# Causal scores in steps of four PSUM banks with one exponential each, two heads sharing a diagonal column, and a new instruction order

## The chip, the core and the metric

The kernel runs on one core of one Trainium2 chip. The core has a matrix engine (TensorE, PE in the profile; its weight loads are PEld), a vector engine (VectorE, DVE), an activation engine (ScalarE, ACT), a general engine (GpSimd, POOL) and a queue of DMA transfers issued by SyncE (SP). Matrix results land in PSUM, which the kernel uses as eight banks of 128 partitions x 512 floats; operands lie in SBUF. Each engine executes its own list of instructions in the order in which the program gives them and waits at an instruction whose operand another engine has not yet finished. The metric is the device time of one execution in microseconds, lower is better, as the median of several runs.

## The reference

Two layers of the same kind run over 2048 tokens of width 512: attention with a compressive memory, then a gated feed-forward network (FFN). The sequence is cut into four segments of 512 tokens, with 32 heads of width 16. Inside a segment attention is causal; what came before enters through a memory matrix per head. The same weights are used in both layers.

```python
def _A_ref(x, wq, wk, wv, wo, beta):
    ...
    mask = (ar[:, None] < ar[None, :]) * -1000000000.0
    g = _sigmoid(beta)
    for s in range(N):
        qs, ks, vs = (q[:, :, s], k[:, :, s], v[:, :, s])
        logits = jnp.einsum('bhqd,bhkd->bhqk', qs, ks) * scale + mask
        a_dot = jnp.einsum('bhqk,bhkd->bhqd', _softmax(logits), vs)
        pq = phi(qs)                       # where(t > 0, t + 1, exp(t))
        num = jnp.einsum('bhld,bhde->bhle', pq, M)
        den = jnp.einsum('bhld,bhd->bhl', pq, z)[..., None] + 1e-06
        outs.append(g * (num / den) + (1.0 - g) * a_dot)
        M = M + jnp.einsum('bhld,bhle->bhde', phi(ks), vs)
        z = z + jnp.einsum('bhld->bhd', phi(ks))
    return o @ wo

x = x + _A_ref(_layernorm(x), ...)
x = x + (_gelu(x1 @ w_gate) * (x1 @ w_up)) @ w_down      # x1 = _layernorm(x)
...                                                       # the same two lines again
```

## The kernel before, in words

**Units of work.** Four segments in two layers make eight units, k = 0 to 7 (`NK`). Unit k first projects its 512 tokens to `q`, `kf` (the keys) and `vaug` (the values with a 17th column for the softmax denominator), then forms causal scores, exponentials and weighted sums, adds the memory part, multiplies by wo, and runs the FFN (wg, wu, wd). The memory state goes from unit to unit, and unit k + 4 needs the finished rows of unit k.

**How the matrix engine is cut.** Dense products (`product`, line 458) run as four instructions on four column strips of 32, so four weight loads and four matmuls make one product of 512 columns. Score matmuls (line 893) use the array in four strips of 32 rows instead, one head in each: even heads read `kf`, odd heads read `kB`, a copy of the odd heads' keys in rows whose other half is zero, so that both kinds contract over their own head only. A change between the two ways of cutting the array is a change of tiling; the planner books `SWITCH` for it. The weighted sums (line 957, called a flush here) are cut into column strips like the dense products.

**Score steps.** The 512 x 512 causal square of one head is covered by four tiles of 128 keys, with 512, 384, 256 and 128 query columns, each tile starting at its diagonal block. Four heads (one parity of the eight heads of a block b of 128 features) go side by side. `steps_of` (line 88) packs the tiles into steps of 512 columns for four heads: 20 steps for each unit (`STEPS`). A step writes 4 x 512 columns in PSUM, in two halves of two banks each (`st0` and `st1`, double use of four fixed banks); `scores` (line 872) can issue both halves together or one half alone. Each half has its own exponential on ACT (line 924, 128 x 1024) into a tile `pt`, and then POOL sets the upper triangle of each diagonal block to zero (line 911). The other four banks (`M_BANKS`) serve all other results.

**Flushes.** When all steps of a head group are exponentiated and masked, `flush_item` (line 932) multiplies `pt` with `vaug`; DVE transposes the result (line 981), divides by the denominator and transposes back.

**The order.** `tc.manual_schedule` is on for all engines: the kernel itself writes out each engine's list. It does so with a planner (`Clocks`, `Engine`, line 123 on, and the loop at line 1316): booked clocks of PE, ACT, DVE, POOL and SP with booked costs, a stock of items (`items`) sorted by due times (`DUE`, `DUE_STEP`, `BIAS`), and score steps that go first whenever their operands and banks are there. Where score steps remain and nothing else is ready, the planner emits a filler: a product of the constant tile `warm` (line 1347), whose result nobody reads. The lists are fixed when the program is built; on the chip each engine goes through its list in order.

**The start.** Lines 355 to 409 fill constants on POOL (`kB` memset at line 401, then `cden` at line 402), 19 matmuls of `warm` run on PE (line 366), and lines 1183 to 1252 write the first normalization, transposes and projections by hand. The POOL list there is: constants, `kB` memset, `cden`, then the scale factors of the first normalization (lines 1196 and 1198).

```python
    def product(out, lhsT, rhs, start=True, stop=True):
        ck.tiling("columns")
        for c in range(4):
            r = slice(32 * c, 32 * c + 32)
            nc.tensor.matmul(out[r], lhsT=lhsT[:, r], rhs=rhs, start=start, stop=stop, tile_position=(0, 32 * c))
```

Of the kernel before, what the change touches and what calls it, by code (L numbers as in the profile page):

```python
# [12 lines left out]
ALU = mybir.AluOpType  # L13
# [5 lines left out]
P = 128  # L19
# [17 lines left out]
STEPS = 20  # L37
BY_PE = {("xnTf", 0), ("xnTf", 1), ("xnTf", NK - 1)}
M_BANKS = 4
PT_STEPS = 5  # L40
SETS = 3
WO, WG, X2, WU, X3, WD = 32.0, 37.0, 14.0, 49.8, 27.0, 94.0
# [4 lines left out]
RAW = 7  # L47
QK_DUE = 0.63
E_Q = -0.37
E_K = 0.716  # L50

FLUSH_WAIT = 6.233
PIECE_SLACK = 1.684
URGENT, SOON, NORMAL = -13.08, -0.462, 0.0
EXP_SLACK, E_SLACK, PHI_SLACK, GELU_SLACK = -2.653, 5.546, 3.783, 2.306
ACT_EVICT, FIRST_EVICT = 0.747, 1.76
XN_BUFS = 4
XN_KEPT = 1
XNA1_PE = 0
E_BUFS = 2  # L60
KB_SLACK = 6.407
# [4 lines left out]
MEM_SLACK = 2.5  # L66


DUE = {"wo": 0.775, "gate": 1.026, "up": 1.341, "down": 1.966, "upd": 0.168, "mem": -0.012, "v": 0.072}
DUE_STEP = {"gate": 0.0137, "up": 0.0202, "down": 0.0455}  # L70
BIAS = {
    **{("qk", k): d for k, d in {0: -0.002, 1: 0.026, 2: 0.13, 3: 0.245, 4: 0.171, 5: 0.126, 6: 0.152, 7: 0.076}.items()},
    **{("mem", k): d for k, d in {0: -0.153, 1: -0.371, 2: -0.114, 3: -0.034, 4: -0.306, 5: 0.161, 6: 0.219, 7: 0.053}.items()},
    **{("down", k): d for k, d in {0: 0.142, 1: -0.173, 2: -0.121, 3: -0.112, 4: 0.005, 5: -0.01, 6: -0.141, 7: -0.221}.items()},
    **{("upd", k): d for k, d in {0: -0.053, 1: 0.405, 2: -0.034, 3: 0.527, 4: -0.125, 5: 0.428, 6: 0.107, 7: 0.051}.items()},
    **{("v", k): d for k, d in {0: 0.15, 1: 0.067, 2: 0.083, 3: 0.486, 4: -0.214, 5: -1.018, 6: -0.01, 7: 0.119}.items()},
    **{("wo", k): d for k, d in {0: 0.143, 1: 0.12, 2: -1.173, 3: -0.74, 4: -0.064, 5: -0.385, 6: 0.174, 7: -0.079}.items()},
    **{("gate", k): d for k, d in {0: 0.569, 1: -0.096, 2: -0.084, 3: 0.003, 4: -0.147, 5: 0.268, 6: -0.122, 7: 0.068}.items()},
    **{("up", k): d for k, d in {0: 0.098, 1: 0.239, 2: 0.148, 3: -0.035, 4: 0.01, 5: -0.013, 6: -0.468, 7: -0.065}.items()},
# [7 lines left out]

def steps_of(k):


    if k not in SPLIT:
        found = []
        for b in range(KT):
            if k == b == 0:
                found += [([(b, par, 0, 0, HALF, HALF * par) for par in range(2)], []),
                          ([(b, par, 0, HALF, L, HALF * par) for par in range(2)], []),
                          ([(b, 0, 1, P, L, 0), (b, 0, 3, 3 * P, L, 3 * P)], []),
                          ([(b, 0, 2, HALF, L, 0), (b, 1, 2, HALF, L, HALF)], [(b, 0, None)]),
                          ([(b, 1, 1, P, L, 0), (b, 1, 3, 3 * P, L, 3 * P)], [(b, 1, None)])]
                continue  # L100
            found += [([(b, 0, 0, 0, L, 0)], []),
                      ([(b, 0, 1, P, L, 0), (b, 0, 3, 3 * P, L, 3 * P)], []),
                      ([(b, 0, 2, HALF, L, 0), (b, 1, 2, HALF, L, HALF)], [(b, 0, None)]),
                      ([(b, 1, 0, 0, L, 0)], []),
                      ([(b, 1, 1, P, L, 0), (b, 1, 3, 3 * P, L, 3 * P)], [(b, 1, None)])]
        return found
    found = []
    for b in (0, 2):
        wide = [[(c, par, 0, 0, HALF, HALF * par) for par in range(2)] for c in (b, b + 1)]
        narrow = [(c, par, 1, P, HALF, P * (2 * (c - b) + par)) for c in (b, b + 1) for par in range(2)]  # L110
        found += [(wide[0], []), (narrow, [(b, None, 0)]), (wide[1], [(b + 1, None, 0)])]
    for b in (0, 2):
        last = [(c, par, 3, 3 * P, L, P * (2 * (c - b) + par)) for c in (b, b + 1) for par in range(2)]
        for c in (b, b + 1):
            for par in range(2):
                found.append(([(c, par, 0, HALF, L, 0), (c, par, 1, HALF, L, HALF)], []))
            found.append(([(c, par, 2, HALF, L, HALF * par) for par in range(2)], [(c, None, 1)] if c > b else []))
            if c == b:
                found.append((last, [(b, None, 1)]))
    return found  # L120
# [53 lines left out]
class Clocks:  # L174
# [4 lines left out]
    SWITCH = 0.102  # L179
# [108 lines left out]
def kernel(  # L288
# [69 lines left out]

    def bank_tile(i, shape, dtype=F32):
        return psp.tile(shape, dtype, tag=f"m{i}", bufs=1, name="m")  # L360
# [28 lines left out]
    bdg = cst.tile([P, 4, P], F32, name="bdg")  # L389
    macc = cst.tile([P, 4, P], F32, name="macc")  # L390
    zacc = cst.tile([P, 4], F32, name="zacc")
    kBs = [cst.tile([P, KT, L], BF16, name=f"kB{i}") for i in range(SETS)]
    vaugs = [cst.tile([P, TPS, VW + 15], BF16, name=f"vaug{i}") for i in range(SETS)]

    def by_head(va):
        return va[:, :, 0:VW].rearrange("p t (h e) -> p t h e", e=DH + 1)
# [6 lines left out]
    for va in vaugs:  # L403
        nc.scalar.activation(out=by_head(va)[:, :, :, DH], in_=cden[:].unsqueeze(1).to_broadcast([P, TPS, H]),
                             func=ACT.Copy)
# [5 lines left out]
    def later_constants():  # L411
# [7 lines left out]
        for b in range(4):  # L419
            ck.pool.post(20.0 + 3.0 * b, MEM_SLACK, (0.5, lambda b=b: scale(b), None))  # L420

# [961 lines left out]
```

## Time and profile before

| what | value |
|---|---|
| time, median of 3 runs | 558.17 us (556.5 to 558.3) |
| span of the profiled execution, first to last instruction | 555.8 us |
| TensorE busy in the span | 547.5 us, 99% |
| ACT / DVE / POOL busy | 447.8 / 434.5 / 233.3 us |
| granted TensorE clock, all slices | 9 tenths or more |
| DMA, mean over the span | 50 GB/s |

The profiled execution is one execution; its span is the time between its first and last profiled instruction, and the measured time of a run also contains what lies around that, about 2.4 us here between the span and the median. Times in the fences are microseconds unless marked ns. In a view of groups the columns after the bar are the busy time of the group, the mean duration of one instruction in ns, and the idle time of the engine before them with what ended it. In a timeline the columns are the start, the duration of a merged piece, the engine, the line, the operation and how many instructions were merged. Matmuls overlap in the pipeline, so that the durations of successive pieces overlap too; what one piece costs is the distance between its start and the start of the next.

### The profile page before, as it was taken

To read this page: it belongs to the slowest core of one execution; us is meant where nothing else is said; L and a number is where in the kernel's file an instruction comes from. 1 tells how busy PE (TensorE), PEld (TensorE's weight loads), DVE (VectorE), ACT (ScalarE), POOL (GpSimd) and SP (SyncE) were. 2 spreads that over 40 slices of the span, in tenths; PEclk is the share of its full clock that TensorE was granted. 3 is DMA by queue.
4 is the path that set the end of the run, shared out by engine and by line. 5 is a ranking of instruction groups with operands and counts; after the bars stand their busy time and mean duration, and the time that the engine had idled before them with its cause. 6 is when DMAs were issued, how large, how long until landed. Compare 5 with 4: busy or idle time off the path is not lost.

```text
span 555.8 us, 25686 instructions
## 1 busy us (share of the span) xinstructions
PE 547.5 (99%) x11557; PEld 272.5 (49%) x11557; DVE 434.5 (78%) x820; ACT 447.8 (81%) x544; POOL 233.3 (42%) x470
## 2 busy tenths in 40 slices
PE   8999999999999999999999999999999999999997
PEld 4433344444454444444444444544454444545996
DVE  5978797999969898687967889489876898587161
ACT  5899999987998878987898978988889877973500
POOL 5675664255624455144632555155632562021000
PEclk9999999999999999999999999999999999999999
DMA  7248710610152024220230205101320104020001
GB/s 228 40 107 220 150 25 13 168 37 2 22 60 50 12 31 69 40 41 2 41 50 12 42 2 86 33 16 28 79 59 3 22 13 87 3 22 31 14 4 40
DMA packets 65261, 27.87 MB, mean 50 GB/s; under 512 B 54720, under 2 KB 64704, under 8 KB 65152
## 3 DMA queue, kind: packets, MB, share of 16 engines
q1 hardware_dynamic: 65008, 26.23, 23.3%
q8 instruction: 90, 1.47, 1.1%
q14 instruction: 19, 0.16, 0.1%
q10 hardware_dynamic: 144, 0.01, 0.0%
HBM read 9.71 MB, written 2.10 MB: 21 GB/s over the span
## 4 chain that ended last, share of the span: by engine, by line
PE 88%; DVE 6%; DMA 2%; POOL 1%; ACT 1%; issue 1%; SPq 0%; ACTq 0%
PE m L463 71%; PE st L893 9%; PE m L957 6%; DVE xn L522 2%; PE m L366 1%; ACT pt L924 1%; DVE byq L981 1%; DVE x_sb L1054 1%; DMA xnT<-xn 1%; DMA amT<-am 1%; POOL rs L509 1%; POOL pt L911 1%; DVE st L486 0%; DVE ab L989 0%; DVE xnT L454 0%
## 5 line engine op out<-in xcount | busy, mean ns | idle before, releaser
L924 ACT ACTIVATE pt<-st 128x1024 bf16<-128x1024 f32 x320 | 309.8, 1026 | 55.5 <-PE st L893 49.8
L911 POOL TENSOR_SCALAR_AFFINE_SELECT pt<-pt 128x256 bf16<-128x256 bf16 (+2 forms) x414 | 204.4, 510 | 265.5 <-ACT pt L924 249.5
L463 PE MATMUL m<-wd_sb,gel 128*32 128x512 bf16 x1792 | 106.1, 380 | 0.4 <-DVE x_sb L1054 0.4
L463 PE MATMUL m<-xnT,wg_sb 128*32 128x512 bf16 (+1 forms) x2016 | 105.4, 356 | 0.8 <-DVE byq L981 0.5
L463 PE MATMUL m<-xnT,wu_sb 128*32 128x512 bf16 (+1 forms) x2016 | 106.0, 356 | 0.1
L1141 DVE TENSOR_TENSOR gel<-gel,m 128x512 bf16<-128x512 bf16 x112 | 75.3, 682 | 34.3 <-PE m L463 31.6
L463 PEld LDWEIGHTS <-wu_sb 128*32 128x32 bf16 x2016 | 52.3, 97 | 40.0 <-issue 4.8
L463 PEld LDWEIGHTS <-wg_sb 128*32 128x32 bf16 x2016 | 51.7, 97 | 39.7 <-issue 5.9
L463 PEld LDWEIGHTS <-gel 128*32 128x32 bf16 x1792 | 50.6, 97 | 40.3 <-issue 5.0
L1054 DVE TENSOR_TENSOR x_sb<-x_sb,m 128x512 bf16<-128x512 bf16 x64 | 42.2, 671 | 22.5 <-PE m L463 22.4
L981 DVE STREAM_TRANSPOSE byq<-m 128x512 f32<-128x512 f32 x64 | 45.2, 706 | 11.5 <-PE m L957 11.4
L957 PE MATMUL m<-pt,vaug 128*32 128x256 bf16 (+3 forms) x1096 | 46.3, 292 | 0.0
L1106 ACT ACTIVATE gel<-m 128x512 bf16<-128x512 f32 x63 | 34.9, 602 | 11.0 <-PE m L463 11.0
L893 PE MATMUL st<-q,kB 32*128 32x256 bf16 (+3 forms) x548 | 41.0, 290 | 0.0
L486 DVE BATCH_NORM_STATS2 st<-x_sb 128x6 f32<-128x512 bf16 x60 | 40.6, 677 | 0.3
L893 PE MATMUL st<-q,kf 16*128 16x256 bf16 (+3 forms) x548 | 39.1, 293 | 0.5 <-ACT q L1228 0.5
L463 PE MATMUL m<-xnT,wq_sb 128*32 128x512 bf16 (+1 forms) x528 | 36.5, 374 | 0.7 <-DVE xnT L564 0.5
L463 PE MATMUL m<-xnT,wk_sb 128*32 128x512 bf16 (+2 forms) x528 | 35.9, 374 | 0.0
L893 PEld LDWEIGHTS <-kf 16*128 16x128 bf16 x548 | 12.2, 91 | 45.5 <-issue 44.3
L957 PEld LDWEIGHTS <-vaug 128*32 128x32 bf16 x1096 | 24.3, 96 | 20.7 <-issue 7.8
L522 DVE TENSOR_SCALAR xn<-x_sb,mv,rs 128x512 bf16<-128x512 bf16 x64 | 29.9, 512 | 2.8 <-POOL rs L509 2.6
L463 PE MATMUL m<-wv_sb,xnT 128*32 128x512 bf16 x512 | 32.1, 380 | 0.0
(91 smaller groups left out, 539.7 us busy)
## 6 DMA issues: line engine op xcount, KB each, us to landing
out_dram<-x_sb SPq DMA_DIRECT2D x16, 128.0 KB, 2.2
wg_sb<-in_B_w_gate_dram SPq DMA_DIRECT2D x8, 224.0 KB, 3.5
kB<-kf SPq DMA_DIRECT2D x28, 64.0 KB, 2.5
wu_sb<-in_B_w_up_dram SPq DMA_DIRECT2D x8, 224.0 KB, 3.9
wd_sb<-in_B_w_down_dram SPq DMA_DIRECT2D x7, 256.0 KB, 3.1
x_sb<-in_A_x_dram SPq DMA_DIRECT2D x3, 512.0 KB, 6.3
xnT<-xn SPq DMA_TRANSPOSE x48, 3.2
x_sb<-in_A_x_dram SPq DMA_DIRECT2D x4, 128.0 KB, 2.8
```

Source lines behind the costliest of these rows:

```text
L366: nc.tensor.matmul(ps[:], lhsT=warm[:], rhs=wide, start=True, stop=True)
L463: nc.tensor.matmul(out[r], lhsT=lhsT[:, r], rhs=rhs, start=start, stop=stop, tile_position=(0, 32 * c))
L486: nc.vector.bn_stats(out=self.st6[:, 0, :], in_=x_sb[:, self.tt0 + j, :])
L522: nc.vector.tensor_scalar(out=xn[:], in0=x_sb[:, self.tt0 + j, :], scalar1=self.mv[:, j, 0:1], scalar2=self.rs[:, j, :], op0=ALU.subtract, ...
L893: nc.tensor.matmul(sts[j // 2][:, j % 2, c0:c0 + q1 - q0], lhsT=lhsT[rows, b, P * ki:P * ki + P], rhs=self.q[rows, b, q0:q1], start=True, ...
L911: nc.gpsimd.affine_select(out=dv, in_=dv, pattern=[[0, w], [1, P]], compare_op=ALU.is_ge, fill=0.0, base=0, channel_multiplier=-1)
L924: 1.024, lambda st=st, tile2=tile2: nc.scalar.activation(out=tile2[:], in_=st[:], func=ACT.Exp, scale=SCALE), told), table="exp")
L957: nc.tensor.matmul(ps()[32 * j:32 * j + 32, q0 + shift:q1 + shift], lhsT=self.vaug[:, ki, h * (DH + 1):h * (DH + 1) + 32], rhs=step["pt"][ ...
L981: nc.vector.transpose(out=self.byq[:, c], in_=ps()[:])
L1054: ck.dve.post(ck.made(), slack, (0.683, lambda: nc.vector.tensor_tensor(out=xt, in0=xt, in1=ps()[:], op=ALU.add), lambda t: (ps.read(t), t ...
L1106: return lambda: nc.scalar.activation(out=out(), in_=in_(), func=ACT.Gelu_apprx_tanh)
L1141: ck.dve.post(ck.made(), NORMAL, (0.683, lambda: nc.vector.tensor_tensor(out=hidden(g, h), in0=hidden(g, h), in1=banked(ps), op=ALU.mult), ...
```

## The change

**Score steps.** All eight PSUM banks become one tile `big`; any four free banks take a step (`four_banks`), the rest serve dense items, up to `CAP` at a time. A step is no longer issued in halves. One exponential of 128 x 2048 covers its four banks if they are evenly spaced.

**Shared columns.** In each diagonal block the first 64 query columns see only the first 64 keys. The change takes these 64 columns out of the ordinary parts. A part of 64 columns with `u == 2` holds two heads: the even head's 64 keys in partitions 0 to 63, the odd head's in partitions 64 to 127, each written by a matmul of its own with 64 key columns. A flush of either head reads this part with `vS`, a copy of the values in which each half of the partitions holds the values of one parity and zeros for the other. 18 steps of 512 columns remain of 20 for most units, two of them made of eight shared parts of 64 columns, 64 matmuls each; unit 7 has its own list.

**Values.** `vaug` is laid out with the 16 even heads first. `vS` is one tile for all units, zeroed once by a memset at the start and filled for each unit by two DMAs from `vaug`, after the last flush of the unit before.

**Gate.** The factor of the memory gate moves from the memory matrix (`bdg`) into the reciprocal of the denominator; `kB` has two buffers in place of three.

**Order.** All due times and slacks of the planner are new, and its booked costs of a step and a tiling change (`STEP`, `PART`, `SWITCH`).

```diff
-M_BANKS = 4
-PT_STEPS = 5
+BANKS = 8
+PT_BUFS = 4
+KB_SETS = 2
+CAP, CAP_FREE = 5, 6
...
+    def shared(blocks, tiles):
+        return [(b, 2, t, P * t, P * t + Q, Q * (len(blocks) * m + n)) for n, b in enumerate(blocks)
+                for m, t in enumerate(tiles)]
...
+    def long(b, par):
+        return [(b, par, 3, L - Q, L, 0), (b, par, 0, Q, L, Q)], []
+
+    def short(b, par, ends):
+        return [(b, par, 1, P + Q, L, 0), (b, par, 2, HALF + Q, L, 320)], ends
...
+            found += [long(b, 0), short(b, 0, []), (shared((b, b + 1), range(TPS)), [(b, 0, None)]),
+                      long(b, 1), short(b, 1, [(b, 1, None)])]
+        for par in range(2):
+            found += [long(b + 1, par), short(b + 1, par, [(b + 1, par, None)])]
...
-    SWITCH = 0.102
+    SWITCH = 0.108
+    STEP, PART = 0.226, 0.012
...
+    big = psp.tile([P, 8, L], F32, tag="big", bufs=1, name="big")
...
     nc.gpsimd.memset(kBs[1][:], 0.0)
+    nc.gpsimd.memset(vS[:], 0.0)
     nc.gpsimd.tensor_scalar(out=cden[:], in0=tmp_e[:], scalar1=1.0, scalar2=None, op0=ALU.add)
...
-        nc.vector.reciprocal(out=tmp_e2[:], in_=tmp_e2[:])
...
+    def may_open():
+        return held("m") < (CAP if step_ready() else CAP_FREE) and len(free_banks()) > 0
...
+                def shared_values(t):
+                    for u in range(2):
+                        c = slice(16 * (DH + 1) * u, 16 * (DH + 1) * (u + 1))
+                        ck.sp.post(t, KB_SLACK, (0.55, lambda u=u, c=c: nc.sync.dma_start(
+                            out=vS[Q * u:Q * u + Q, :, c], in_=self.vaug[0:Q, :, c]),
+                            lambda t2, u=u: ck.at(t2 + 1.8, lambda: ev.update({("vS", k, u): t2 + 2.0 + KB_MARGIN}))))
...
+                    va = vS if u == 2 else self.vaug
                     for j in range(4):
                         nc.tensor.matmul(ps()[32 * j:32 * j + 32, q0 + shift:q1 + shift],
+                                         lhsT=va[:, ki, values_of(va, b, p, j)],
+                                         rhs=step["pt"][:, j, c0:c0 + q1 - q0], start=n == 0,
+                                         stop=n == len(pieces) - 1, tile_position=(0, 32 * j))
...
+                for (lhsT, rows), cols, p0 in todo:
+                    width = cols.stop - cols.start
+                    nc.tensor.matmul(big[p0:p0 + width, got[j], c0:c0 + q1 - q0], lhsT=lhsT[rows, b, cols],
+                                     rhs=a.q[rows, b, q0:q1], start=True, stop=True, tile_position=(32 * j, p0))
+        ck.tiling("rows")
+        begun = ck.pe
+        ck.on_pe(ck.STEP + ck.PART * (len(parts) - 2))
...
+        for g in groups:
+            banks_of = got[g]
+            st = big[:, banks_of[0]:banks_of[-1] + 1:banks_of[1] - banks_of[0], 0:width]
+            ck.act.post(max(ready, step["at"]), EXP_SLACK, (
+                0.172 + 0.000832 * width * len(banks_of), lambda g=g, st=st: nc.scalar.activation(
+                    out=pt[:, g, 0:width], in_=st, func=ACT.Exp, scale=SCALE), lambda t, g=g: told(t, g, g is groups[-1])),
+                table="exp")
```

More of the change, by code (lines that the diff above doesn't have):

```diff
@@ L85 @@
 EARLY = 1
+Q = P // 2
 def steps_of(k):
[L91 to L105, printed above, removed]
-        return found
@@ new lines, in step_ready, with four_banks @@
+    def step_ready():
+        if not streams:
+            return False
+        k, t, parts, _ = streams[0]
+        names = set()
+        for b, u, *_ in parts:
+            names.add(("q", k, b))
+            if k or t > 1:
+                names |= {("k", k, b)} | ({("kB", k, b)} if u else set())
+        return ck.has(*names, by=ck.pe - 0.055) and not room_of(parts).full()
+    def four_banks():
+        free = free_banks()
+        if len(free) < 4:
+            return None
+        for first in (4, 0, 3, 2, 1):
+            if all(first + i in free for i in range(4)):
+                return [first + i for i in range(4)]
+        for got in ([0, 2, 4, 6], [1, 3, 5, 7]):
+            if all(i in free for i in got):
+                return got
+        return free[-4:]
```

449 lines of the change are left out of this document (241 added, 208 removed).

## The prediction

> **What bounds the kernel now.** I read the page first: the busy shares, the slices and the chain that ended last.
>
> ```profile
> PE 547.5 (99%) x11557; PEld 272.5 (49%) x11557; DVE 434.5 (78%) x820; ACT 447.8 (81%) x544; POOL 233.3 (42%) x470
> ...
> PE   8999999999999999999999999999999999999997
> ...
> PEclk9999999999999999999999999999999999999999
> DMA  7248710610152024220230205101320104020001
> ...
> PE 88%; DVE 6%; DMA 2%; POOL 1%; ACT 1%; issue 1%; SPq 0%; ACTq 0%
> ```
>
> TensorE is busy in every slice, at the full granted clock, and 88% of the chain that ended last is its own. The view of waits says how much of the rest is waiting:
>
> ```profile
> PE m L366 <- DVE warm L357: 1.1, 1, 1.1
> PE m L463 <- DVE byq L981: 0.8, 3, 0.5
> PE m L463 <- DVE x_sb L1054: 0.6, 2, 0.4
> PE m L463 <- DVE xnT L454: 0.5, 2, 0.3
> ```
>
> Apart from 1.1 us at the very start no cause reaches 1 us in total. So the time is the sum of what TensorE's list costs, and a change counts by what it adds to that list or takes from it, and by waits that it newly puts in front of it. ACT's 81% costs nothing by itself; work that leaves ACT is worth nothing until it lets TensorE's list get shorter.
>
> Busy time does not give an instruction's price, as successive matmuls overlap. I take prices from the distance between starts in the timeline of TensorE. First a whole step, a flush and dense products:
>
> ```profile
> 201.32 0.40 PE L893 MATMUL st<-q,kf 16*128 16x384 bf16 x8
> 201.65 0.73 PE L957 MATMUL m<-pt,vaug 128*32 128x512 bf16 x16
> 202.20 1.90 PE L463 MATMUL m<-wd_sb,gel 128*32 128x512 bf16 x32
> 204.03 0.29 PE L893 MATMUL st<-q,kf 16*128 16x256 bf16 x4
> 204.15 0.28 PE L893 MATMUL st<-q,kB 32*128 32x256 bf16 x4
> 204.36 1.05 PE L463 MATMUL m<-wd_sb,gel 128*32 128x512 bf16 x16
> 205.24 1.04 PE L463 MATMUL m<-xnT,wq_sb 128*32 128x512 bf16 x16
> ```
>
> Four products of 512 columns take 205.24 - 204.36 = 0.88 us, with the first one after a step a little dearer; at 0.216 us each the eight products from 202.20 end at 203.93. The step starts at 204.03, and the next products at 204.36. So a visit to the scores costs 0.10 before it and 0.33 in it, some 0.435 us, of which the columns (512, as in a product of 0.216 us) are half; the other half is the two changes of tiling. A flush of 1280 columns costs 202.20 - 201.65 = 0.55 us. Second, a step that was issued in halves:
>
> ```profile
> 35.05 0.39 PE L893 MATMUL st<-q,kf 16*128 16x512 bf16 x2
> 35.37 0.61 PE L463 MATMUL m<-xnT,wq_sb 128*32 128x512 bf16 x8
> 35.91 0.39 PE L893 MATMUL st<-q,kf 16*128 16x512 bf16 x2
> 36.23 0.40 PE L463 MATMUL m<-xnT,wq_sb 128*32 128x512 bf16 x4
> ```
>
> Each half costs 0.32 us itself, as much as a whole step, because two heads stream their 512 columns in the time of four.
>
> **The change, part by part.**
>
> *Visits.* Both programs are built, so that their lists can be counted. Before, TensorE's list enters the scores 181 times: 160 steps, 21 of them in halves. After, it enters 144 times: 128 ordinary visits and 16 with shared columns, each of 64 matmuls of 64 key columns and 64 query columns. Before: 181 x 0.435, less 42 x 0.01 for the halves, 78.3 us. After, ordinary: 128 x 0.435 = 55.7 us.
>
> A shared visit has no row. Its 512 column-slots would stream in 0.21 us if both halves of the key columns run side by side in the eight strips. The nearest rows are the smallest matmuls there are, the memory denominators, in groups of four:
>
> ```profile
> 88.95 0.68 PE L463 MATMUL m<-zcols,phiq 128*32 128x8 bf16 x64
> 89.47 1.05 PE L463 MATMUL m<-xnT,wg_sb 128*32 128x512 bf16 x16
> ```
>
> 64 of them take 0.52 us, though their eight columns are a 64th of a product's. A list of 64 matmuls with a weight load each thus costs up to 0.52, whatever it streams. That is the upper end and 0.21 the lower; I take 0.40, nearer to the row, because a visit begins behind long products and the first instructions stand ready. With the tiling changes 0.62 each: 16 x 0.62 = 9.9 us. Visits after: 65.6 us, a gain of 12.7. The ends of the shared visit move this by -3.0 and +1.9.
>
> The new ordinary steps begin with a part of 64 columns (0.027 us) ahead of one of 448; the weights of the long part then load behind a short one. Before, the longer part came first. For 70 such parts I add 0.9 us, between nothing and 2.2 (all as dear as 0.056 us, a quarter of the 0.216 product).
>
> *Flushes.* The columns stay the same, 1280 for each flush. The pieces go from four to eight: 326 groups of four matmuls with 64 columns. The flush above costs 0.55 us, and its columns alone 1280 / 512 x 0.216 = 0.54, so a group has a fixed cost of a few ns: +0.8 us. At the denominators' 0.033 us for a group (0.52 / 16) instead of 0.027 (0.216 / 8) it is +2.0; below nothing cannot be, as the columns are the same.
>
> *Fillers.* They show where the planner found nothing to do.
>
> ```profile
> L463 PE MATMUL m<-warm x80: 379/379/391, 25.3 to 76.7; 128*32 128x512 bf16 x80
> ```
>
> 80 matmuls are 20 products, all before 77 us, while unit 0 and unit 1 are the only work and the FFN weights are still coming. The new list has 224, 56 products, nearly all ahead of the first gate product too: 36 x 0.216 = +7.8 us. This takes back more than half of the gain. It is the price of longer chains where little else is there: one exponential for four banks, a shared visit of which two blocks wait for masks on POOL, and `vS`. It is a count from the list, so I give it no range.
>
> *Start.* The memset of `vS` stands on POOL behind that of `kB` and ahead of the first scale factors.
>
> ```profile
> 2.55 1.80 POOL L401 MEMSET kB<- 128x2048 bf16 x1
> 4.45 0.30 POOL L402 TENSOR_SCALAR cden<-tmp_e 128x32 bf16<-128x32 f32 x1
> 5.30 0.23 POOL L1196 TENSOR_SCALAR ve<-mv 128x2 f32<-128x2 f32 x1 [0.55 <-DVE mv L1193]
> 5.61 0.72 POOL L1198 TENSOR_TENSOR rs<-ve,mhalf 128x2 f32<-128x2 f32 x1
> 6.72 0.70 DVE L522 TENSOR_SCALAR xn<-x_sb,mv,rs 128x512 bf16<-128x512 bf16 x2
> 7.26 0.62 PE L561 MATMUL m<-ident,xn 128*128 128x128 bf16 x8
> ```
>
> 2236 elements at 1.80 us for 2048 are 1.97 us. `cden` moves to about 6.4, `ve` to 6.7, `rs` ends near 7.7, and the first normalized rows start on DVE near 7.75 instead of 6.72. TensorE waits for them at its first transposes, and every list is behind that: +1.0 us (0.7 to 1.1; the second pair of rows moves by 0.7, and DVE loses a reciprocal of 0.35 there). The planner's start times are written by hand and unchanged, so its lists do not know of this.
>
> *Off the path.* ACT gets lighter; the exponentials and masks of before:
>
> ```profile
> L924 ACT ACTIVATE pt<-st 128x1024 bf16<-128x1024 f32 x320 | 309.8, 1026 | 55.5 <-PE st L893 49.8
> L911 POOL TENSOR_SCALAR_AFFINE_SELECT pt<-pt 128x256 bf16<-128x256 bf16 (+2 forms) x414 | 204.4, 510 | 265.5 <-ACT pt L924 249.5
> ```
>
> 145 exponentials of twice the size cost at most 2 x 1.026 us each, 297.5 us in all against 320 x 1.026 = 328.3. POOL has 337 selects in place of 414, some of 16 x 64 elements on half of the partitions, with room at 42%. The gate's move adds nothing: the same six denominator instructions and a copy fewer on POOL. All this is hidden behind TensorE's list; uncovered it would show as waits at the flushes, which is a rival below.
>
> *Sum.* -12.7 + 0.9 + 0.8 + 7.8 + 1.0 = -2.2 us. The profiled execution's span of 555.8 becomes 553.6, with what lies around it left at the 2.4 us that part span and median: **556.0 us** against 558.2. With all ends taken together the case itself reaches from 552 to 559; I hold 553.5 to 558.5 as its own range.
>
> [...] The row of the kf weight loads, and the products beside it:
>
> ```profile
> L893 PEld LDWEIGHTS <-kf 16*128 16x128 bf16 x548 | 12.2, 91 | 45.5 <-issue 44.3
> ```
>
> A load shows 0.091 us, yet 64 denominators, whose strips share all rows, take 0.52 us together: their loads are hidden behind matmuls of the same rows. [...]
>
> **The rivals.**
>
> *Small pieces hide.* The shared visit streams in 0.21 us, the first parts and flush pieces cost only columns: -3.0 - 0.9 - 0.8 from the forecast, **551.3 us**. For it: the ready instructions behind long products. Against it: the 0.52 us row.
>
> *The hand-over of `vS` becomes a wait (the other side).* `vS` is a single tile. It can be filled only after the last flush of the unit before, by two DMAs in SP's queue, which stands still while a DMA's sources are not done; behind them wait the transposes of `xnT` and `phik`. All flushes of a unit, and with them its step buffers, wait for it, and TensorE's list is fixed.
>
> ```profile
> kB<-kf SPq DMA_DIRECT2D x28, 64.0 KB, 2.5
> ...
> x_sb<-in_A_x_dram SPq DMA_DIRECT2D x3, 512.0 KB, 6.3
> ```
>
> A copy of 136 KB lands between 2.5 and 6.3 us; the planner books 0.55 + 2.0 + 1.5 = 4.05. Late by 1.0 us in each of eight units it costs 8 us: **564 us**. It decides from (2.2 + 1.7) / 8 = 0.5 us for each unit. For it: a new chain through POOL, SP and DMA in front of a list that never waited. Against it: the middle of the two rows is near what is booked, and after the first six slices the DMA engines are mostly idle.
>
> *The shared visit doesn't do what it says.* If the key halves do not run side by side, or the list supplies them no faster than the denominators, a shared visit gives 0.52 + 0.22 us: 16 x 0.12 = +1.9, **557.9 us**, within what can be told from no change.
>
> [...]
>
> **How the numbers follow.** Forecast 0.42, small pieces hidden 0.17, late `vS` 0.26, shared visits at 0.52 us 0.10, loads exposed 0.05. 0.3% of 558.2, about what can be told from no change, is 1.7 us: faster means below 556.5, slower above 559.9. The forecast's own range lies on both sides of 556.5 and gives 0.24 faster and 0.18 same; small pieces 0.17 faster; late `vS` and exposed loads 0.31 slower; shared visits 0.07 same, 0.03 slower. Together faster 0.41, same 0.25, slower 0.34. The range reaches from the fast rival, a little below it, to the slow side short of the last rivals: 550 to 563.
>
> **What would show it.** In the new profile: visits to the scores 0.33 us from start to next start for ordinary steps and near 0.51 for shared ones; flushes near 0.56; the first `xn` on DVE near 7.75 us; a `warm` group of 224 matmuls; ACT below 430 us busy. The waits of TensorE should stay near 1 us for each cause. It is wrong if a wait for `vS`, for masks or for exponentials of several us stands in that view, if the shared visits lie outside 0.21 to 0.52 without the tiling changes, or if the start is not later. A time below 550 would mean that fillers or waits went that I count as fixed; one above 563 a second cause beside `vS`.

## The result and the profile after

| kernel | median | runs from to | ratio to the kernel before, 95% interval |
|---|---|---|---|
| before, beside it | 557.36 us | 556.5 to 558.3 | |
| changed | 571.51 us | 571.41 to 572.24 | 1.0253 [1.0235, 1.0271] |

The change makes the kernel 2.5% slower, where 556.0 us were forecast with a range of 550 to 563. The spans of the profiled executions are 555.8 and 569.7 us, 13.9 us apart. From the page of the changed kernel: busy time of the engines, and TensorE's busy tenths in 40 slices.

```profile
PE 548.6 (96%) x13741; PEld 290.2 (51%) x13741; DVE 438.6 (77%) x823; ACT 413.0 (73%) x365; POOL 216.5 (38%) x389
...
PE   7988989999999999999999999999999999999997
PEclk9999999999999999999999999999999999999999
...
L1314 ACT ACTIVATE pt<-big 128x2048 bf16<-128x2048 f32 (+1 forms) x145 | 270.7, 1867 | 81.1 <-PE big L1245 70.6
```

ACT has 35 us less to do, as it was to be, and the granted clock is 0.998 on the mean, with 9 tenths or more in every slice. TensorE is busy for as long as before, but in a longer span. Of the first six slices, up to 85 us, four are not full, where before only the very first was not. The view of TensorE's waits (total, times, longest, in us), whose causes were all below 1 us before except the first:

```profile
PE big L504 <- ACT pt L1314: 5.1, 4, 2.0
PE big L949 <- ACT pt L1314: 1.8, 1, 1.8
PE big L1245 <- ACT pt L1314: 1.7, 2, 0.9
PE big L504 <- DVE x_sb L1047: 1.4, 2, 1.0
PE big L504 <- issue: 1.4, 3, 0.8
PE big L602 <- DVE xn L563: 1.1, 1, 1.1
...
PE big L949 <- issue: 1.0, 1, 1.0
```

Exponentials (L1314) make 8.6 us of it. The surprising row is the first: L504 are dense products, which read nothing that an exponential makes. They can wait for one only because of the bank that they write.

The same two stretches in both kernels (start:end, length, busy time and instructions of PE, PEld, DVE, ACT and POOL, clock, share and rate of the DMA), first the kernel before, then the changed one:

```profile
20.00:60.00 40.00, 40.00 (x688) 15.95 (x684) 34.51 (x68) 37.28 (x47) 25.65 (x57) 1.00 0.62 141
60.00:100.00 40.00, 39.56 (x866) 18.37 (x866) 33.05 (x63) 38.87 (x50) 19.56 (x39) 1.00 0.29 66
```

```profile
20.00:60.00 40.00, 34.86 (x828) 16.71 (x820) 30.04 (x64) 26.94 (x29) 15.45 (x36) 1.00 0.58 133
60.00:100.00 40.00, 35.59 (x1032) 18.65 (x1023) 32.02 (x65) 32.66 (x28) 21.57 (x35) 1.00 0.76 143
```

In these 80 us TensorE stands idle for 9.1 us more, though its list holds more fillers here than before. ACT tells why it is a different regime: before it worked for 76 of the 80 us, now for 60. The exponentials alone, in the same 80 us (length, busy time and count), before and after:

```profile
20.00:100.00 80.00, 55.42 (x58) 1.00 0.46 104
```

```profile
20.00:100.00 80.00, 41.87 (x24) 1.00 0.67 138
```

58 halves are 29 steps; now there are 24. The scores, which were the work that filled TensorE while the FFN could not yet begin, come later, and the FFN with them. The rows of the gate products (TensorE, durations in ns, then the first and the last start in us), before and after:

```profile
L463 PE MATMUL m<-xnT,wg_sb x2016: 269/379/391, 81.3 to 528.1; 128*32 128x512 bf16 x143, 128*32 128x256 bf16 x41
```

```profile
L504 PE MATMUL big<-xnT,wg_sb x2016: 269/379/390, 102.5 to 541.0; 128*32 128x512 bf16 x143, 128*32 128x256 bf16 x41
```

The first gate product starts 21 us later than before.

### The profile page after: what moved, and what is told of

Read it like the earlier page. It is cut to its first block, busy times and chain, and to the rows that moved or that the text cites. A ratio compares the mean times of both kernels' runs of the same rounds, so it can differ in the third digit from the quotient of the medians.

```text
span 569.7 us, 29845 instructions
## 1 busy us (share of the span) xinstructions
PE 548.6 (96%) x13741; PEld 290.2 (51%) x13741; DVE 438.6 (77%) x823; ACT 413.0 (73%) x365; POOL 216.5 (38%) x389
## 4 chain that ended last, share of the span: by engine, by line
PE 85%; DVE 5%; POOL 4%; ACT 3%; issue 2%; DMA 1%; ACTq 0%; DVEq 0%; POOLq 0%
PE big L504 71%; PE big L1245 8%; PE big L949 6%; POOL pt L1287 2%; ACT pt L1314 2%; DVE e L780 1%; DMA phik<-e 1%; DVE x_sb L1047 1%; DVE byq L974 1%; DVE phiq L761 1%; DVE gel L1134 1%; DVE xn L563 0%; POOL vS L445 0%; POOL kB L444 0%; DVE e L788 0%
## 5 line engine op out<-in xcount | busy, mean ns | idle before, releaser
L1314 ACT ACTIVATE pt<-big 128x2048 bf16<-128x2048 f32 (+1 forms) x145 | 270.7, 1867 | 81.1 <-PE big L1245 70.6
L1287 POOL TENSOR_SCALAR_AFFINE_SELECT pt<-pt 64x256 bf16<-64x256 bf16 (+3 forms) x337 | 188.1, 582 | 286.0 <-ACT pt L1314 282.5
L504 PE MATMUL big<-wd_sb,gel 128*32 128x512 bf16 x1792 | 106.9, 380 | 1.9 <-DVE x_sb L1047 1.0
L504 PE MATMUL big<-xnT,wg_sb 128*32 128x512 bf16 (+1 forms) x2016 | 105.6, 356 | 0.2 <-issue 0.2
L504 PE MATMUL big<-xnT,wu_sb 128*32 128x512 bf16 (+1 forms) x2016 | 104.6, 356 | 0.5 <-issue 0.3
L1134 DVE TENSOR_TENSOR gel<-gel,big 128x512 bf16<-128x512 bf16 x112 | 75.4, 683 | 35.1 <-PE big L504 31.1
L504 PEld LDWEIGHTS <-wu_sb 128*32 128x32 bf16 x2016 | 52.4, 97 | 40.6 <-issue 3.8
L504 PEld LDWEIGHTS <-wg_sb 128*32 128x32 bf16 x2016 | 51.5, 97 | 40.2 <-issue 5.4
L504 PEld LDWEIGHTS <-gel 128*32 128x32 bf16 x1792 | 49.2, 97 | 42.7 <-issue 7.9
L1047 DVE TENSOR_TENSOR x_sb<-x_sb,big 128x512 bf16<-128x512 bf16 x64 | 42.4, 676 | 28.4 <-PE big L504 28.1
L974 DVE STREAM_TRANSPOSE byq<-big 128x512 f32<-128x512 f32 x64 | 45.1, 705 | 11.6 <-PE big L949 8.5
L949 PE MATMUL big<-pt,vaug 128*32 128x192 bf16 (+4 forms) x1096 | 45.1, 266 | 1.1 <-issue 1.0
L1245 PE MATMUL big<-q,kf 16*64 16x64 bf16 (+5 forms) x1060 | 37.8, 235 | 2.2 <-ACT pt L1314 1.7
L504 PE MATMUL big<-xnT,wq_sb 128*32 128x512 bf16 (+1 forms) x528 | 35.6, 374 | 3.7 <-ACT pt L1314 3.1
L504 PE MATMUL big<-xnT,wk_sb 128*32 128x512 bf16 (+2 forms) x528 | 35.0, 373 | 2.0 <-ACT pt L1314 2.0
L504 PE MATMUL big<-wv_sb,xnT 128*32 128x512 bf16 x512 | 31.7, 380 | 0.4 <-DVE x_sb L1047 0.4
L504 PE MATMUL big<-wo_sb,aT 128*32 128x512 bf16 x512 | 31.6, 380 | 0.0
```

Of the source, the lines that this page charges most:

```text
L949: nc.tensor.matmul(ps()[32 * j:32 * j + 32, q0 + shift:q1 + shift], lhsT=va[:, ki, values_of(va, b, p, j)], rhs=step["pt"][:, j, c0:c0 + q ...
L974: nc.vector.transpose(out=self.byq[:, c], in_=ps()[:])
L1047: ck.dve.post(ck.made(), slack, (0.683, lambda: nc.vector.tensor_tensor(out=xt, in0=xt, in1=ps()[:], op=ALU.add), lambda t: (ps.read(t), t ...
L1134: ck.dve.post(ck.made(), NORMAL, (0.683, lambda: nc.vector.tensor_tensor(out=hidden(g, h), in0=hidden(g, h), in1=banked(ps), op=ALU.mult), ...
L1245: nc.tensor.matmul(big[p0:p0 + width, got[j], c0:c0 + q1 - q0], lhsT=lhsT[rows, b, cols], rhs=a.q[rows, b, q0:q1], start=True, stop=True, ...
L1287: nc.gpsimd.affine_select(out=v, in_=v, pattern=[[0, m], [1, size]], compare_op=ALU.is_ge, fill=0.0, base=0, channel_multiplier=-1)
```

## The experiments

The theory after the result was: the counted list is about right, and the loss is waits, of which the largest part are the dense products that wait for exponentials. In the changed kernel, ScalarE and TensorE around the first of these waits:

```profile
35.20 1.88 ACT L1314 ACTIVATE pt<-big 128x2048 bf16<-128x2048 f32 x1 [0.79 <-DVE byq L974]
```

```profile
34.80 0.82 PE L504 MATMUL big<-xnT,wk_sb 128*32 128x512 bf16 x12
37.13 1.05 PE L504 MATMUL big<-xnT,wq_sb 128*32 128x512 bf16 x16 [1.51 <-ACT pt L1314]
```

The step at 35.20 took banks 1, 3, 5 and 7. Its exponential began only when VectorE had read a flush's result (`byq`) from a bank between them, and ended at 37.08; the product at 37.13, in another bank between them, began 0.05 us later. Four steps in a row (unit 0) took odd banks in this way. In the program such a strided operand is ordered as the range from its first bank to its last: the products wait for a semaphore of ScalarE.

**Single-bank exponentials for the strided steps (e1).** All lists stay as they are; only these four exponentials become four of one bank.

```diff
+        def powers(g, st, banks_of):
+            if banks_of[1] - banks_of[0] == 1:
+                nc.scalar.activation(out=pt[:, g, 0:width], in_=st, func=ACT.Exp, scale=SCALE)
+                return
+            for n, i in enumerate(banks_of):
+                nc.scalar.activation(out=pt[:, g.start + n, 0:width], in_=big[:, i, 0:width], func=ACT.Exp, scale=SCALE)
...
-                0.172 + 0.000832 * width * len(banks_of), lambda g=g, st=st: nc.scalar.activation(
-                    out=pt[:, g, 0:width], in_=st, func=ACT.Exp, scale=SCALE), lambda t, g=g: told(t, g, g is groups[-1])),
+                0.172 + 0.000832 * width * len(banks_of), lambda g=g, st=st, banks_of=banks_of: powers(g, st, banks_of),
+                lambda t, g=g: told(t, g, g is groups[-1])),
```

> Engine lists as in the changed kernel, except that the four exponentials that read every second bank are written as four exponentials of one bank each (ACT pays about 4 x 0.6 us instead of 1.87). Theory A (a strided read counts as its whole range of banks, so that evictions and products in the banks between are ordered with it): the four waits of TensorE at 37 to 47 us (1.67, 0.65, 1.28 and 2.19 us beyond the next start) go, and the time falls by 4 to 6 us, to about 566. Rival B (those banks were truly needed and ACT was late): the longer ACT work makes it slower, 571 to 574.

Measured: 565.05 us (564.66 to 567.12), ratio 1.0150 [1.0127, 1.0174]; span 563.2, that is 6.5 us less. Its waits:

```profile
PE big L949 <- ACT pt L1312: 1.8, 1, 1.8
PE big L504 <- DVE x_sb L1047: 1.4, 2, 1.0
PE big L1245 <- ACT pt L1312: 1.4, 2, 0.8
PE big L504 <- issue: 1.2, 2, 0.8
PE big L504 <- DMA phik<-e: 1.2, 2, 0.8
```

The row of products that wait for exponentials is gone, although ScalarE now takes longer for such a step (four in 2.06 us against one in 1.88). It could still be that four short exponentials only gave their banks back one by one, earlier than a long one. The rows of e1 for the second of the four steps, which is 64 columns wide, speak against it:

```profile
37.66 0.61 ACT L1315 ACTIVATE pt<-big 128x64 bf16<-128x64 f32 x4
```

```profile
37.45 0.82 PE L504 MATMUL big<-xnT,wq_sb 128*32 128x512 bf16 x12
```

The product that waited until 40.02 in the changed kernel is the second of these three. It starts at 37.66, together with the first of the four exponentials and before any of them has ended. So 6.5 of the 13.9 us are false waits on banks that nobody shares.

**The late memset (e2, e3, e5, e9).** The memset of `vS` moves behind the first scale factors on GpSimd (e2, and e3 on top of e1), to VectorE behind the memset of `warm` (e5, on e1), and there with fewer `warm` matmuls (e9).

```diff
-    nc.gpsimd.memset(vS[:], 0.0)
+    nc.vector.memset(vS[:], 0.0)
...
-WARM = 19
+WARM = 15
```

> Only the memset of vS moves on POOL, from ahead of cden to behind the first scale factors. Theory A (the start is 1 us late and all of TensorE's list stands behind it): first xn on DVE at 6.7 us instead of 7.8, first transposes at 7.3 instead of 8.3, time 1.0 us lower, 570.5. Rival B (the early waits and transfers set the pace there, the delay is absorbed): same start, but time unchanged within 0.3 us.

> Both edits. If the two causes are separate and additive: 571.5 - 5 - 1 = 565. What then remains above the kernel before (557.4) is about 8 us, to be looked for in the shared visits and in waits that are not in the early strided steps. If one hides the other: 566 to 567.

> The kernel of e1 (single-bank exponentials where the four banks are not neighbours), with the memset of vS on VectorE behind the memset of warm, where VectorE has nothing to do until about 3.7 us, in place of GpSimd. Theory A (the list is behind the start, so that a late first normalization is late everywhere): the scale factors on GpSimd start again near 5.3 us, the first xn on VectorE at 6.7 to 6.8 in place of 7.8, the first transposes near 7.3, and the last matmul is 1.0 us earlier than in e1: 564.0 us (e1 565.05). Theory B (later waits, for loads or VectorE, take up the lead): the first transposes near 7.3, but no more than 0.3 us less at the end: 564.8 to 565.1. If VectorE's memset and GpSimd's constants slow one another as in e2, the first xn comes later than 7.0.

> The kernel of e5 with 15 matmuls of warm at the start in place of 19, since in the profile of e5 the first transposes waited for them until 8.18 us though xn was there at 7.2. Theory A (a late start is late everywhere): the transposes start at 7.2 to 7.4 and the time is 0.8 to 1.0 us below that of e1, near 564 us. Theory B (the lead is lost at later waits): the transposes start as early, and the time stays within 0.4 us of e1 and e5, 565 to 567 us. If the matmuls that follow run at half their pace longer because fewer came before, the rows of the first 12 us show it.

Measured: e2 572.11 us (ratio 1.0300 [1.0249, 1.0352]), e3 567.37 (1.0185 [1.0168, 1.0201]), e5 566.89 (1.0144 [1.0116, 1.0173]), e9 565.08 (1.0127 [1.0100, 1.0155]). None of e2, e3 and e5 is faster than the kernel that it starts from. In e2 the later memset fell together with a long instruction of VectorE, in the rows of both:

```profile
7.08 0.70 DVE L562 TENSOR_SCALAR xn<-x_sb,mv,rs 128x512 bf16<-128x512 bf16 x2
...
8.43 2.02 DVE L562 TENSOR_SCALAR xn<-x_sb,mv,rs 128x512 bf16<-128x512 bf16 x1 [0.53 <-POOL rs L1335]
...
10.85 0.41 DVE L562 TENSOR_SCALAR xn<-x_sb,mv,rs 128x512 bf16<-128x512 bf16 x1
```

```profile
8.35 1.96 POOL L1347 MEMSET vS<- 128x2236 bf16 x1
```

The instruction of 0.41 us took 2.02 beside the memset and ended 0.14 us after it. How the one held up the other is not shown. In e5 `xn` was begun at 6.73, as in the kernel before (6.72), and yet the first transposes began at 8.18:

```profile
1.11 7.24 PE L405 MATMUL big<-warm 128*128 128x512 bf16 x19 [1.11 <-DVE warm L383]
8.18 0.61 PE L601 MATMUL big<-ident,xn 128*128 128x128 bf16 x8
```

The 19 `warm` matmuls stood in front. At the start they come every 0.43 us, and later every 0.216; the change came at 4.8 us in the profile of the changed kernel and as late as 7.3 in e5's. With 15 of them (e9):

```profile
1.10 6.25 PE L405 MATMUL big<-warm 128*128 128x512 bf16 x15 [1.10 <-DVE warm L383]
7.26 0.72 PE L601 MATMUL big<-ident,xn 128*128 128x128 bf16 x8
```

The transposes are back at the 7.26 of the kernel before, and the ratio falls from e1's 1.0150 to 1.0127, some 1.3 us, but the intervals overlap. That the late start is worth about 1 us is possible and not shown.

**Shorter columns in shared visits (e4).** The 64 matmuls of a shared visit stream 16 columns in place of 64, so that three quarters of the scores of these visits are not computed.

```diff
-                    nc.tensor.matmul(big[p0:p0 + width, got[j], c0:c0 + q1 - q0], lhsT=lhsT[rows, b, cols],
-                                     rhs=a.q[rows, b, q0:q1], start=True, stop=True, tile_position=(32 * j, p0))
+                    n = 16 if u == 2 and len(parts) == 8 else q1 - q0
+                    nc.tensor.matmul(big[p0:p0 + width, got[j], c0:c0 + n], lhsT=lhsT[rows, b, cols],
+                                     rhs=a.q[rows, b, q0:q0 + n], start=True, stop=True, tile_position=(32 * j, p0))
```

> The matmuls of the 16 shared visits stream 16 query columns instead of 64, the rest of those score columns isn't computed; count and weights unchanged. Theory A (a list of 64 small matmuls with a weight load each is supplied no faster than about 8.3 ns per pair): a shared visit stays at 0.62 to 0.64 us from start to next start. Rival B (the two key halves don't run side by side, each streams its 64 columns after the other): it falls to 0.40 or below.

Measured: 568.84 us in one run, span 567.1. The shared visit of 64 matmuls in the changed kernel, its first rows and its last, with the products around it:

```profile
201.03 0.39 PE L504 MATMUL big<-xnT,wu_sb 128*32 128x512 bf16 x4
201.35 0.21 PE L1245 MATMUL big<-q,kf 16*64 16x64 bf16 x1
201.35 0.21 PE L1245 MATMUL big<-q,kB 32*64 32x64 bf16 x1
...
201.84 0.21 PE L1245 MATMUL big<-q,kB 32*64 32x64 bf16 x1
201.98 1.26 PE L504 MATMUL big<-xnT,wu_sb 128*32 128x512 bf16 x20
```

From its first matmul to the next product it takes 0.63 us, with a quarter of the columns 0.59 (201.47 - 200.88, the same distance in the trace of e4), a little below theory A's figure and far above rival B's 0.40. Its 64 matmuls begin within 0.49 us, 8 ns each. So its price is hardly what they stream, as theory A has it; what holds the 64 at 8 ns each was not tested apart. For 16 visits that is 0.6 us; that this one run is 2.7 us shorter than the changed kernel is not explained by it. Ahead of it, the product at 201.03 needs 0.216, which leaves the 0.10 of the tiling change that ordinary visits have too.

**No fillers (e8).** The order of e1 without its 56 filler products.

```diff
-                product(ps()[:], warm[:], wide)
+                ck.tiling("columns")
```

> The kernel of e1 with the same order of all other work, but without the 56 filler products (224 matmuls) that the order puts where the planner had nothing else; a result that nobody reads is left out. The prediction counted 36 more fillers as 7.8 us of cost. Theory A (they are work in the list like any other, and what stands behind them is ready early): up to 56 x 0.216 = 12.1 us go, 553 to 558 us. Theory B (they stand where what follows waits for an exponential, a mask or a load anyway): the time falls by less than 3 us, 562 to 565 us, and the waits of TensorE grow by what the fillers took. If the granted clock falls below 1.00 in the stretches of 20 to 100 us, that is a third effect, and the products there take longer than 0.216 us.

Measured: 565.87 us (564.6 to 567.62), ratio 1.0137 [1.0105, 1.0169], no difference from e1 that the intervals show. Its waits:

```profile
PE big L1245 <- ACT pt L1312: 4.0, 3, 2.1
PE big L949 <- POOL pt L1287: 2.6, 5, 1.3
PE big L504 <- DVE x_sb L1047: 2.1, 3, 1.0
```

All rows of waits sum to 17.4 us, against 10.2 in e1: some 7 of the fillers' 12 us turned into waits for exponentials, masks and x. The rest would be the third effect that the expectation names. Two stretches of e8, in which e1 has a granted clock of 1.00:

```profile
20.00:35.00 15.00, 13.69 (x308) 6.95 (x304) 13.11 (x32) 10.08 (x15) 9.16 (x20) 0.89 0.66 105
...
65.00:80.00 15.00, 10.94 (x258) 5.08 (x257) 9.03 (x16) 10.36 (x8) 5.19 (x12) 0.77 1.05 179
```

Their clocks of 0.89 and 0.77 are worth some 5 us, by an estimate of (0.11 + 0.23) x 15 that takes the work to stretch as the clock falls. The mean clock is 0.986 to 0.991 in all four runs, against 0.998 to 1.000 in e1. So these fillers cost nothing on balance: they stand where TensorE would wait, and without them the clock was granted less. A count of fillers is a count of waits that the planner foresaw, and leaving them out does not win the prediction's +7.8 back.

**Other orders (e6, e7).** In e6 the planner books the measured price of a shared visit and takes neighbouring banks only; e7 has no shared columns, no `vS`, and five `pt` tiles. Both have due times and slacks found anew.

```diff
+        ck.on_pe(ck.STEP + ck.PART * (len(parts) - 2) if not halves else 0.0083 * 8 * len(parts))
...
-        for got in ([0, 2, 4, 6], [1, 3, 5, 7]):
-            if all(i in free for i in got):
-                return got
-        return free[-4:]
+        return None
```

> The changed kernel with another order: the planner books a shared visit of 64 matmuls at 0.53 us without the change of tiling, as the run of the change showed it, takes only four neighbouring banks for a step, and its due times and slacks were found anew for that. Its list has 143 visits, 16 of them shared, and 46.5 filler products in place of 56. By the prices measured, against the kernel before: visits -11.1, fillers 26.5 x 0.216 = +5.7, start +1.0: -4.4 us without waits. Theory A (the new waits are those of an order found for prices that the chip does not have): TensorE's idle time falls from 16 to about 5 us and the time is 554 to 557 us. Theory B (waits belong to whole steps on four banks and their one exponential, whatever the order): 10 us or more of idle time stay, as in e1, and the time is 560 to 564 us.

> The changed kernel without shared columns: the 20 steps of 512 columns that the kernel before has for a unit, no vS, five pt tiles, whole steps with one exponential on four neighbouring banks, due times and slacks found anew for it. Its list has 158 visits to the scores, none of 64 matmuls, and 61 filler products. By the prices measured, against the kernel before: visits 23 x 0.435 = -10.0 us, and fillers 41 x 0.216 = +8.9: -1.1 us without waits, and a start as before. Theory A (the shared columns bring the loss): 556 to 559 us. Theory B (whole steps on four banks bring it): idle time of TensorE of 8 us or more, 561 to 566 us. Beside e6 this says whether the sharing pays at all: by theory A of e6 the kernel with shared columns is some 3 us ahead.

Measured: e6 569.98 us (568.88 to 570.95), ratio 1.0207 [1.0172, 1.0241]; e7 565.74 us (564.15 to 566.56), ratio 1.0134 [1.0104, 1.0164]. In both the idle time is that of theory B: behind its first matmul TensorE stands idle for 16.7 and 11.5 us (3.6 in the kernel before, 9.7 in e1). The time of e7 lies in theory B's range; that of e6 lies 6 us above it, and by ratio or median 3 to 5 us above e1, which stays unexplained. e6 had no strided step and the right price, and waits elsewhere:

```profile
PE big L1242 <- ACT pt L1311: 2.6, 3, 1.8
PE big L504 <- DMA phik<-e: 2.5, 1, 2.5
PE big L504 <- DVE byq L974: 2.2, 1, 2.2
```

e7 loses as much as e1 with no shared column in it, so a loss of this size does not need the sharing. But e6 and e7 have an order of their own, and e6 against e1 shows that two orders of nearly the same work can differ by 3 to 5 us.

**Whole steps alone (e10), and two exponentials for a step (e12).** e10 is the kernel before, with its four fixed banks and two exponentials, but no half steps, and due times found anew. e12 is e1 with every exponential of neighbouring banks cut in two.

```diff
-        return (0,) if free[0] and (idle and k >= HALF_FROM or k < HALF_STEPS and not other) else ()
+        return ()
```

> The kernel before with one part of the change alone: a step is never issued in halves. Four fixed banks, two exponentials of 128 x 1024, no shared columns, and due times and slacks found anew for it, as for e6 and e7. Its list has 160 visits in place of 181 and 100.5 filler products in place of 20. By prices: 21 x 0.435 = -9.1 us of visits, 80.5 x 0.216 = +17.4 us of fillers, +8.3 us in all. Theory A (the half steps kept TensorE fed in the first 100 us, and giving them up costs more than their changes of tiling): 565 to 568 us, with the fillers between 20 and 100 us, and idle time of TensorE near the 3.6 us of the kernel before. Theory B (the loss of the changed kernel comes from the common pool of banks or from the shared columns, and whole visits pay): below 559 us, which would need the fillers to cover waits that the kernel before has too.

> The kernel of e1 with the same lists, but two exponentials of 128 x 1024 for a step where it had one of 128 x 2048; two banks come free 0.9 us earlier, and ScalarE has about 130 x 0.17 = 22 us more to do. Theory A (the length of the one exponential makes the waits): TensorE's waits for exponentials (1.8 and 1.4 us in e1) fall to about half and the time by 1 to 2 us, to 563 to 564 us. Theory B (the waits come from steps that need four banks at once): a score step waits for the second exponential as long as before, and the time stays within 0.7 us of e1's 565.05, or rises where ScalarE is late.

Measured: e10 574.05 us (569.75 to 574.91), ratio 1.0250 [1.0201, 1.0298]; e12 566.25 us (565.8 to 567.3), ratio 1.0138 [1.0114, 1.0162], no difference from e1. The fillers of e10 (the durations, then the first and last start), and its stretch from 60 to 100 us in two fences:

```profile
L463 PE MATMUL m<-warm x400: 376/379/628, 24.3 to 169.0; 128*32 128x512 bf16 x134
```

```profile
60.00:100.00 40.00, 36.32 (x804) 17.39 (x796) 31.40 (x63) 32.35 (x43) 18.48 (x36) 0.91 0.68 134
```

With one small part of the change, and an order found anew for it, the kernel before loses as much as with the whole change: its span is 573.1 us, 17.3 more than before. The list gives 8.2 of it (21 visits fewer, -9.1; 80 more filler products, +17.3). The rows of waits give 3.5 more (7.8 in sum, 4.3 before), and the granted clock of 0.91 in the 40 us shown some 3.6, by the same kind of estimate, 0.09 x 40; 2 us stay open. The one run of e10 with a mean clock of 1.000 took 569.75 us, 11 more than the kernel before. The direction is that of theory A, the size nearly twice what it expected, and not all fillers stand where it expected them: 45 of the 100 products come after 128 us. As the order was found anew, e10 does not part the half steps from the order. The run that would do so, the kernel before with its half steps and an order found in the same way, was not made.

In e12 the time does not fall, and the longest wait for an exponential remains; the waits of score steps for one fall from 1.4 to 0.9 us:

```profile
PE big L949 <- ACT pt L1313: 1.9, 1, 1.9
```

## Why the prediction was wrong

*The start* was right: `xn` at 7.80 us (7.75 forecast) and the transposes at 8.27, 1.0 us late. Whether that reached the end was not shown (e9).

```profile
7.80 0.74 DVE L563 TENSOR_SCALAR xn<-x_sb,mv,rs 128x512 bf16<-128x512 bf16 x2 [1.02 <-POOL rs L1336]
```

*Ordinary visits* were right, and a little better. The rows of an ordinary visit that begins with a part of 64 columns, in the changed kernel, and of a flush in e1:

```profile
44.47 0.40 PE L1245 MATMUL big<-q,kB 32*128 32x64 bf16 x8
44.80 0.61 PE L504 MATMUL big<-xnT,wk_sb 128*32 128x512 bf16 x8
```

```profile
41.89 0.20 PE L949 MATMUL big<-pt,vS 128*32 128x64 bf16 x4
...
42.44 1.47 PE L504 MATMUL big<-warm 128*32 128x512 bf16 x24
```

0.33 us as before, with the first part of 64 columns in it, so the 0.9 us for first parts fall away. A flush of eight pieces takes 0.55 us, as one of four did: the 0.8 us fall away too.

*Shared visits* were mis-sized. The forecast took 0.40 us without the tiling changes, between 0.21 and 0.52, because the first instructions stand ready. With them it was to cost 0.62 us, and costs 0.10 + 0.63 = 0.73; that is the price of the denominators (0.52 + 0.22), and readiness at the visit's beginning buys nothing. This is the rival in which the shared visit doesn't do what it says: 16 x 0.11 = +1.8 us. Without the tiling changes the visit lies at the upper end of the bounds given. The chances also count exposed loads, with 0.05; no run shows that term. The 64 loads of the visit at 201.35 show 0.10 us each and begin within 0.50 us, and the visit's own part takes 0.63.

*The hand-over of `vS`*, the rival on the slow side, did not happen:

```profile
vS<-vaug SPq DMA_DIRECT2D x16, 136.0 KB, 3.1
```

The copies land in 3.1 us, inside what is booked, and none of the rows of waits of the changed kernel names `vS` (in e5 one does, with 0.2 us). SP's queue did stand still at these copies until flushes were done, for 24.8 us in four waits. Whether later transfers were late by it was not tested apart; e7, which has no `vS`, loses as much as e1. The forecast's side was wrong for another reason than the one named.

*The step that failed* is the sentence on what counts: "by what it adds to that list or takes from it, and by waits that it newly puts in front of it". The sum held the first and left the second at nothing but the start. "Off the path" called the exponentials hidden and promised a rival for the case that they are not; none of the rivals is that one. The prediction's own sign of being wrong, a wait for exponentials of several us, stands in the view with 8.6. With the measured prices the list is shorter by 3.1 us (visits -12.7 + 1.8 = -10.9, fillers +7.8), with the start by 2.1; the span grew by 13.9, so new waits are 16 us. Of these 6.5 are the four strided exponentials (shown by e1). They could have been read in the changed program: a pool of banks that hands out 1, 3, 5 and 7 makes one operand of a range that other work lies in.

The other 9.5 us stay in e1, and their cause is argued, not shown. In e1's own order neither shorter exponentials (e12) nor leaving out the fillers (e8) brings them down. In orders of their own, a loss of this size is there without the shared columns (e7) and with their price booked right (e6), and a larger one without half steps in the banks of before (e10). What these kernels have in common is that every step is whole; but they also have in common an order found anew. A half step can begin when two banks are free; a whole step needs four at once. In the trace of before, 33 of the 42 half visits lie ahead of 100 us, in the stretch where the changed kernel stands idle. The FFN begins late in all of them: the first gate product starts at 96.6 us in e1, 91.2 in e7 and 99.1 in e10, against 81.3 before. The prediction counted the 21 split steps as 21 x 0.435 = 9.1 us to be saved. By this reading it should have counted them as what stood in place of waits. The fillers showed part of this (+7.8), the rest comes as waits on the chip.

What stays open: behind its first matmul TensorE stands idle for 16.1 us against 3.6 before, which with the 1.1 us for `xn` leaves 11.4 for the 16. A wait may cost more than it shows, as a product of 512 columns is drawn for 0.38 us and the next could follow after 0.216, but that was not measured apart. And e6, e7 and e10 each hold one order; a better one for whole steps may exist. No kernel tried beats the kernel before.

One slip of the prediction decided nothing: its "552 to 559" for all ends together is too narrow, as the ends that it lists itself reach from 551.0 to 560.5.

## What to carry to other kernels

Before removing an extra visit or a split step, ask what the engine would have done in its place: in a list that is full to 99%, the small pieces may be there because the large one could not start. Where a pool hands out buffers, look at which combinations it can form, and whether one instruction over them is ordered against what lies between. Count fillers as waits that are known, and ask for those that are not: here 16 us of new waits came on top of 7.8 us of new fillers.

## What the hardware showed beyond that

The moment from which `warm` matmuls start every 0.216 us in place of 0.43 lay at 4.8 us in the profile of the changed kernel and at 7.3 us in that of e5, though both began them at 1.11 us. The profile's row of the granted clock reads 1.00 all that time, so that it does not show this change. The two moments lie 3.7 and 6.2 us after the first matmul; what sets them is not shown. The 19 take 6.03 us in the changed kernel and 7.17 in e1, whose lists begin alike. A start that is tuned to a tenth of a microsecond is thus at the mercy of about 1 us here, as in e5 (transposes at 8.18 in place of 7.26).

64 matmuls with 16 columns take 0.59 us (e4), only 0.04 us less than 64 with 64 columns, and 64 with 8 columns took 0.52 us in the kernel before: at these widths the columns hardly set the price.
